# Wo gradient: first operands fetched into the space of the finished row sums, output rows during the weight gradients, SwiGLU backward loads in order of need

## The chip, the cores and the metric

One core of one Trainium2 chip. The metric is the device time of one execution in microseconds (us), lower is better. Medians are over the runs of one kernel.

## The reference, cut to what matters

The program is the forward pass and the gradients of `x + s * g`, where `s` is a recurrent attention with memory over segments of 32 rows (32 heads of 128) and `g` is a SiLU of a SwiGLU block. bfloat16, 2048 rows, width 640, hidden width 1728.

```python
def _fwd_reference(...):
    xn = _layernorm(x)
    s = _A_ref(xn, A_mem0, A_Wq, A_Wk, A_Wv, A_Wo, A_seg_len)    # recurrent, 64 segments of 32 rows
    g = _silu(_B_ref(xn, B_w1, B_w3, B_w2))                     # SwiGLU: (silu(x w1) * (x w3)) w2
    return x + s * g
# outputs: x + s * g (out_0) and the gradients for x, mem0, Wq, Wk, Wv, Wo, w1, w3, w2
```

What follows the recurrent part matters here: the gradients of Wq, Wk, Wv (matmuls `wg`), of Wo (`oa`), of w2 (`w2a`), the SwiGLU backward blocks (`pghb`, `pgxb`), and the gradients of w1 and w3 (`wa`).

## The kernel before: the parts that the change touches

Loads and stores are issued by an engine's queue: `nc.sync` is SP, `nc.scalar` is ScalarE, `nc.gpsimd` is GpSimd. A `tag` names a space in SBUF; a pool's space is free when its `with` block ends. `in_order(k, start)` keeps the instructions of a stage as written, engine by engine; where it is not called, a scheduler chooses their order within each engine.

```python
def phase6_Awgrads(k, out3, out4, out5):           # weight gradients, 8 passes (called quarters) x 22 units
    ...
        hr = hp.tile([120, NTL, D], BF16, name="hr")              # 3.2 MB
        acc = hp.tile([P, NW, D], F32, name="ghacc")              # row sums, 51 KB per partition
        ...
        ld(0); ld_w(0); ld(1); ld(2)     # one statement per line in the kernel
        nc.scalar.dma_start(hr[:, 0:NTL - 1, :], ...)
        ...
        for qd in range(8):
            for tl in range(NTL): ...                             # units
            for i in range(3):
                wg(qd, i) ...                                     # three sweeps of matmuls
        in_order(k, start)

def phase6b_gWo(k, out0, out6, gz):                # Wo gradient
        def ep_ld(tt):
            for nm_, src in (("s", k.SR), ("g", k.GB), ("x", k.A_x), ("G", k.G), ("dz", k.DZ)):
                t_ = io.tile([P, D], BF16, name=f"ep_{nm_}", tag=f"ep_{nm_}")      # two buffers
                nc.gpsimd.dma_start(t_[:], src[rows, :])
        def ep(tt):
            nc.vector.tensor_tensor(g, s, g, ALU.mult)
            nc.vector.tensor_tensor(g, g, x, ALU.add)
            nc.scalar.dma_start(out0f[tt * P:tt * P + P, :], g)                  # output rows
            nc.vector.tensor_tensor(G, G, s, ALU.mult)
            nc.vector.tensor_tensor(gz[:, tt, :], G, dz, ALU.mult)
        ...
        for qd in range(8):
            # orr (2.6 MB) on SP's queue; with qd == 0 also gow (3.3 MB) on ScalarE's queue
            for jp in range(2):
                tt = 2 * qd + jp
                ep_ld(tt + 1)                                     # if there is one
                ep(tt)
                # 80 matmuls oa <- orr, gow; then per head: VectorE and ScalarE copy half
                # of it each to wgoo, SP stores it

def phase5_Bbwd_ln(k, out0, out1, out6, out7, out8, out9):
        for t0 in range(0, NT, 4):
            nc.scalar.dma_start(hb[:, t0:t0 + 4, :], ...)         # 7.1 MB in all
        nc.scalar.dma_start(w2T[:], ...)                          # 2.2 MB
        phase6b_gWo(k, out0, out6, gz)
        ...                                                       # w2a; staging of three buffers
        nc.scalar.dma_start(xn_all[:], ...)                       # 2.6 MB
        for b0 in range(0, S, BLK):                               # eight SwiGLU blocks
            ...   # per pair of chunks: load SLT and DUT tiles (three buffers), pghb matmuls,
            ...   # VectorE: ggT = pghb * du, guT = pghb * sl; then pgxb, transposes, layer norm
```

## Time and profile before

| what | us |
|---|---|
| median | 5746.97 (5737.85 to 5747.56, 4 runs) |
| span of the profiled run | 5743.5 |
| first transpose of the weight gradients (`t`) to first `g` matmul | 42.4 |
| first `g` matmul to the end of the last `wg` | 1470.7 |
| end of the last `wg` to the first `oa` | 53.8 |
| `oa`, first to last | 197.9 |
| to the end of the last `w2a` | 73.7 |
| to the first long run of `pgxb` (the entry of the SwiGLU blocks) | 27.2 |
| SwiGLU blocks, to the first `wa` | 241.8 |
| `wa` to the end | 122.3 |
| sum from the first `t` on | 2229.8 |

The rows are cut where TensorE goes from one kind of matmul to the next, read from its timeline. I use this ledger for every run, because the 3500 us before the first `t` scatter: it began at 3499 to 3532 us in the runs of this study, and no experiment touches what lies ahead of it.

The prediction shows the holes. In the list of waits of VectorE and GpSimd for 5026 to 5280 us (us in total, times, longest), products of the output rows wait for their loads, and a load waits for the store of an older output row:

```profile
DVE ep_g L1489 <- DMA ep_g<-GB: 59.0, 12, 41.9
DVE ep_G L1492 <- DMA ep_s<-SR: 21.5, 11, 5.8
POOL ep_g L1483 <- DMA out_dram<-ep_g: 60.0, 10, 37.9
```

### The profile page before, as it was taken

The numbers are of one execution on the slowest core, as the hardware profiler recorded it, in microseconds if no ns is written. First come the engines' busy times: TensorE is split into PE (matmuls) and PEld (weight loads), VectorE is DVE, ScalarE is ACT, GpSimd is POOL, SyncE is SP. The second block draws the span as 40 slices with busy tenths as digits, with TensorE's granted clock in tenths as the row PEclk, the third lists the DMA queues.
The fourth block names the chain that finished last, engine by engine and source line by source line (L and its number), as shares of the span: only waits on it lengthen the run. The fifth ranks groups of instructions, "written<-read, shape, count | busy, mean of one in ns | idle before, by whom it ended". The sixth has DMA issues, their size and how long they took to land. (4 is left out here: it accounts for less than half of the span.)

```text
span 5743.5 us, 166838 instructions
## 1 busy us (share of the span) xinstructions
PE 5004.5 (87%) x67332; PEld 3202.8 (56%) x67614; DVE 2395.4 (42%) x7479; ACT 1838.9 (32%) x5045; POOL 1530.8 (27%) x2536
## 2 busy tenths in 40 slices
PE   5959799999999775898888986999999999959899
PEld 2536455555555444565556554566556665537565
DVE  5824455555555423444444442233223332221351
ACT  2424355555555422333333322233222322201111
POOL 0000144444444302333333333233223322120000
PEclk9969899999999786999999997999999999979999
DMA  6565355555555565666666655243333433284332
GB/s 221 161 245 197 108 158 157 160 160 157 158 150 147 143 180 160 171 180 186 173 176 176 174 159 116 74 110 91 95 81 93 108 86 83 73 291 134 103 118 89
DMA packets 1011244, 833.21 MB, mean 145 GB/s; under 512 B 506030, under 2 KB 899538, under 8 KB 1007156
## 3 DMA queue, kind: packets, MB, share of 16 engines
q1 hardware_dynamic: 759999, 574.71, 35.6%
q0 software_dynamic: 88176, 133.83, 8.4%
q10 hardware_dynamic: 162297, 113.98, 6.7%
q8 instruction: 533, 8.73, 0.7%
q14 instruction: 239, 1.96, 0.1%
HBM read 509.18 MB, written 324.39 MB: 145 GB/s over the span
## 5 line engine op out<-in xcount | busy, mean ns | idle before, releaser
L1407 PE MATMUL wg<-gr,hr 120*128 120x512 bf16 (+1 forms) x2640 | 590.0, 384 | 17.6 <-DVE dST L1339 12.9
L1385 PE MATMUL g<-w,gT 128*128 128x320 bf16 x3840 | 547.5, 299 | 0.0
L1407 PEld LDWEIGHTS <-hr 120*128 120x128 bf16 (+1 forms) x2640 | 258.3, 99 | 341.3 <-issue 48.5
L1385 PEld LDWEIGHTS <-gT 128*128 128x128 bf16 x3840 | 368.4, 98 | 135.8
L250 POOL DMA_DIRECT2D r<-GOS x256 | 143.0, 561 | 925.3 <-PE r6p L1349 876.3
L373 PEld LDWEIGHTS <-gkv 128*8 128x8 bf16 x8192 | 217.1, 100 | 159.7 <-DVE gkv L1048 35.1
L90 DVE CAST wgo<-wg 128x512 bf16<-128x512 f32 x72 | 47.5, 688 | 585.7 <-PE wg L1407 293.8
L354 PEld LDWEIGHTS <-hx 128*32 128x32 bf16 x7680 | 177.9, 96 | 164.6 <-issue 4.5
L90 DVE CAST stg<-bank 128x512 bf16<-128x512 f32 x256 | 177.2, 692 | 200.3 <-PE bank L354 186.6
L373 PE MATMUL gbank<-WvT,gkv 128*8 128x320 bf16 x4096 | 236.2, 410 | 28.1 <-DVE gkv L1048 28.1
L663 ACT ACTIVATE xP<-xsp,xnm 120x120 bf16<-120x120 f32 (+1 forms) x704 | 240.6, 376 | 10.1 <-DVE xnm L659 5.1
L1518 PE MATMUL oa<-gow,orr 128*128 128x320 bf16 x1280 | 180.9, 305 | 70.8 <-DMA gow<-GWO 55.5
L1394 DVE TENSOR_TENSOR ghacc<-ghacc,g 128x320 f32<-128x320 f32 x240 | 117.2, 488 | 283.8 <-PE g L1385 283.8
L92 ACT CAST wgo<-wg 128x512 bf16<-128x512 f32 x48 | 25.8, 589 | 637.8 <-PE wg L1407 637.8
L1352 ACT CAST gr<-r6p 120x512 bf16<-120x512 f32 (+1 forms) x176 | 103.2, 587 | 373.9 <-PE r6p L1349 337.8
L1185 POOL DMA_DIRECT2D DSR<-gdS x176 | 100.9, 573 | 412.1 <-DVE gdS L1183 391.1
L712 POOL DMA_DIRECT2D OR<-xv x163 | 94.8, 582 | 404.7 <-ACT xv L711 284.9
L92 ACT COPY gT<-t6g 128x960 bf16<-128x960 bf16 (+5 forms) x216 | 167.0, 792 | 111.2 <-PE t6g L1368 110.7
L674 POOL TENSOR_TENSOR xP<-xP,xrz 120x480 bf16<-120x480 bf16 x163 | 161.9, 994 | 140.1 <-ACT xP L663 90.9
L1518 PEld LDWEIGHTS <-orr 128*128 128x128 bf16 x1280 | 127.5, 100 | 124.4 <-issue 72.3
L1183 DVE SCALAR_TENSOR_TENSOR gdS<-gdp,Dx,gPr 120x120 bf16<-120x120 f32 (+1 forms) x704 | 188.8, 330 | 0.0
L1180 DVE CUSTOM_DVE_ANT_0 gdS<-gdp,gPr 120x120 bf16<-120x120 f32 (+1 forms) x704 | 153.7, 274 | 62.3 <-PE gdp L1169 52.2
(335 smaller groups left out, 11113.4 us busy)
## 6 DMA issues: line engine op xcount, KB each, us to landing
QVS<-stg SPq DMA_DIRECT2D x128, 256.0 KB
gqv<-QVS SPq DMA_DIRECT2D x112, 192.0 KB
vTt<-VTD SPq DMA_DIRECT2D x64, 320.0 KB
orr<-OR SPq DMA_DIRECT2D x16, 1280.0 KB
VTD<-gvT POOLq DMA_DIRECT2D x168, 120.0 KB, 3.4
OR<-xv POOLq DMA_DIRECT2D x163, 120.0 KB, 2.6
DSR<-gdS POOLq DMA_DIRECT2D x168, 112.5 KB, 3.2
dS<-DSR SPq DMA_DIRECT2D x168, 112.5 KB
```

The costliest lines, as they stand in the source:

```text
L90: return nc.vector.tensor_copy(out, in_)
L92: return nc.scalar.copy(out, in_)
L250: eng.dma_start(d, src if src.shape[0] > 1 else src[0])
L354: k.nc.tensor.matmul(bank[32 * g:32 * g + 32, :], x[:, dc, :], W[:, dc, c0:c0 + 512], start=(dc == 0), stop=(dc == k.DC - 1), tile_positio ...
L373: k.nc.tensor.matmul(pm[p0:p0 + nq, 0:320], x[:, h, :], W[:, h, 320 * b:320 * b + 320], start=(first and i == 0), stop=(last and i == 15), ...
L663: nc.scalar.activation(Pb[0:n, j, 0:n], sp[0:n, j, :], ACT.Exp, bias=nmx[0:n, j:j + 1], scale=k.scale, accum_out=Z[0:n, j:j + 1])
L674: eng.tensor_tensor(Pb[0:n, :, 0:n], Pb[0:n, :, 0:n], bc_last(rz[0:n], n), ALU.mult)
L1180: nc.vector.tensor_tensor_reduce(dS[0:n, j, :], dp[0:n, j, :], Pr[0:n, j, :], 1.0, 0.0, ALU.mult, ALU.add, Dx[0:n, j:j + 1])
L1183: nc.vector.scalar_tensor_tensor(dS[0:n, j, :], dp[0:n, j, :], Dx[0:n, j:j + 1], Pr[0:n, j, :], op0=ALU.subtract, op1=ALU.mult)
L1385: nc.tensor.matmul(pg[:], ring[:, i, j, r0:r0 + P], Ws[qd][i][:, j, 320 * h:320 * h + 320], start=(i == 0 and j == 0), stop=(i == 2 and j ...
L1407: nc.tensor.matmul(accs[dc][:], hr[0:n, tl, dc * P:(dc + 1) * P], st["g", NTL * qd + tl, i][0:n, :], start=(tl == 0), stop=(tl == NTL - 1))
L1518: nc.tensor.matmul(ac[j][i][:], orr[:, w, jj * P:(jj + 1) * P], gow[:, w, 320 * i:320 * i + 320], start=(w == 0), stop=(w == NW - 1))
```

## The change

Its intent: close TensorE's hole before the Wo gradient by fetching gow and the first orr early, into space that is no longer used (the row sums move to a pool of their own); take work out of that stage that could be done elsewhere (the output rows); and put every large load at the time at which it is needed. The diff, cut to its core:

```diff
 def phase6_Awgrads
-        acc = hp.tile([P, NW, D], F32, name="ghacc")
+        acc = X.tile([P, NW, D], F32, name="ghacc", tag="x")
...
                 s4(u)
+                if tl % 11 == 2:
+                    out_ld(2 * qd + tl // 11)        # s, g, x on GpSimd's queue, one buffer each
+                if tl % 11 == 6:
+                    out_rows(2 * qd + tl // 11)      # two VectorE products, store on GpSimd's queue
...
+            else:                                    # last quarter, ahead of its three sweeps
+                xg = X.tile([P, NW * (D + 512)], BF16, name="xg", tag="x")
+                ...
+                    nc.scalar.dma_start(gow[...])
+                    nc.sync.dma_start(orr[...])
 def phase6b_gWo
-            for nm_, src in (("s", k.SR), ("g", k.GB), ("x", k.A_x), ("G", k.G), ("dz", k.DZ)):
+            for nm_, src in (("s", k.SR), ("G", k.G), ("dz", k.DZ)):
...
+        rows_ld(1)                                   # orr 1; later rows_ld(qd + 2) after each qd
...
                 ep(tt)
+                if qd > 1 and late:
+                    nc.scalar.dma_start(*late.pop(0))  # one of nine slices of hb and w2T
...
+        in_order(k, start)
 def phase5_Bbwd_ln
-            nc.scalar.dma_start(hb[...])             # and w2T: at once, ahead of gow
+            late.append((hb[...]))                   # and w2T: handed to phase6b_gWo
...
-            w1T, w3T, gzT in a pool of their own
+            x5 = X.tile([P, 2 * FC * D + DC * NT * P], BF16, name="x5", tag="x")
...
-                        ot = op.tile([P, 320], BF16, name="w2o", tag="w2o")        # three buffers
+                        ot = op.tile([P, 320], BF16, name="w2o", tag="w2o", bufs=7)
...
-            nc.scalar.dma_start(xn_all[:], ...)
+                        nc.gpsimd.dma_start(xn_all[:, b0 // P:b0 // P + 2, :], ...)  # per block
```

## The prediction

> **What bounds the kernel now.** The change touches only what comes after the recurrent part: the weight gradients (from about 3510 us), the Wo gradient (matmuls named oa), the SwiGLU backward pass (gzp, w2a, pghb, pgxb) and the last two weight gradients (wa). I read the page first for the limiting engine, then the chain of waits from 5000 us on, a table of engine busy time by stage, TensorE's list of waits, and last the timeline around each hole.
>
> ```profile
> PE 5004.5 (87%) x67332; PEld 3202.8 (56%) x67614; DVE 2395.4 (42%) x7479; ACT 1838.9 (32%) x5045; POOL 1530.8 (27%) x2536
> ```
>
> TensorE is the busiest by far; the other engines have more than half the span free. A gain here is a hole of TensorE closed. The stage table puts edges where the matmul groups begin and end:
>
> ```profile
> core 0: us, PE busy (x) PEld busy (x) DVE busy (x) ACT busy (x) POOL busy (x), PEclk, DMA share, GB/s
> 5026.80:5080.60 53.80, 0.00 (x0) 0.02 (x1) 7.09 (x14) 0.44 (x1) 11.81 (x22) 0.52 1.03 368
> 5080.60:5278.50 197.90, 180.91 (x1280) 127.53 (x1280) 38.84 (x83) 11.58 (x31) 30.88 (x58) 0.96 0.56 181
> 5278.50:5352.20 73.70, 70.38 (x529) 46.66 (x528) 10.81 (x24) 10.34 (x20) 0.00 (x0) 1.00 0.28 89
> 5352.20:5367.60 15.40, 2.35 (x11) 1.35 (x10) 1.46 (x5) 0.85 (x2) 0.00 (x0) 0.66 0.73 237
> ```
>
> Row one is the hole between the last weight gradient and the first oa matmul: 53.8 us without a matmul, DMA engines full at 368 GB/s. Row four is a second hole of 15.4 us before the SwiGLU blocks. Who ended them:
>
> ```profile
> PE oa L1518 <- DMA gow<-GWO: 55.5, 2, 53.8
> PE oa L1518 <- DVE wgoo L1523: 15.1, 3, 8.5
> PE pghb L1761 <- DVE w2o L90: 8.1, 1, 8.1
> PE pgxb L1774 <- DVE ggT L1763: 5.8, 2, 5.0
> ```
>
> And why gow came so late (start, duration, engine, instruction, idle before it):
>
> ```profile
> 5026.86 12.41 ACTq L1706 DMA_DIRECT2D hb_all<-HB  x4
> ...
> 5029.34 0.69 DVE L90 CAST wgo<-wg 128x512 bf16<-128x512 f32 x1 [2.04 <-DMA out_dram<-wgo]
> ...
> 5060.20 0.37 ACTq L1708 DMA_DIRECT2D w2T<-W2T  x1
> 5060.61 9.25 ACTq L1506 DMA_DIRECT2D gow<-GWO  x2
> ...
> 5080.61 7.26 PE L1518 MATMUL oa<-gow,orr 128*128 128x320 bf16 x40 [53.84 <-DMA gow<-GWO]
> ...
> 5089.49 20.67 PE L1518 MATMUL oa<-gow,orr 128*128 128x320 bf16 x151 [1.62 <-DMA gow<-GWO]
> ```
>
> No load could start before the weight gradients gave up their space at 5026.8. Then ScalarE's queue took hb (7.1 MB, wanted at 5279) and w2T (2.2 MB, wanted at 5360) ahead of gow (3.3 MB, wanted at once). The first 40 oa matmuls run at 181 ns each, the next 151 at 137 ns: the clock was cold too.
>
> [...] granted clock 0.52 in the long hole, and 181 against 137 ns after it. So a hole costs its length plus a cold start. [...] That bears on the output-row loads, which move into the weight gradients on GpSimd's queue. In the trace such loads beside the same VectorE ops (0.49 us each) land in 2.9 to 6.1 us[...].
>
> **The change part by part.**
>
> (1) gow and the first orr (3.3 + 2.6 MB) go into the space of the row sums ghacc, free once the last row sum is added at about 4955 us. 72 us of weight-gradient matmuls follow, at a DMA share of 0.06. At 368 GB/s they take 16 us: hidden. The listing of the changed kernel's waits shows what the first oa matmul then waits for: these loads, and the evacuation of the last accumulators, the last being VectorE's third wgo copy. Before, that copy ran 5029.34 to 5030.03, because its staging buffer waited 2 us for a store; nothing changes there. New start of oa 5030.1, hole 3.3 us, gain 80.6 - 30.1 = 50.5 us.
>
> (2) Inside oa. 1280 matmuls at 136.9 ns (20.67/151) are 175 us; the stage took 197.9. The 23 us more are the cold start, the second half of gow (1.6 us) and 15.1 us behind VectorE's wgoo copies. [...]its copies stood behind output-row products whose loads waited for stores that had themselves queued on ScalarE behind hb and gow. The change takes those products out (two of four per row tile), fetches only three row loads instead of five, writes the order down, and puts one slice of hb per row tile after the fourth. A row tile lasts 175/16 = 10.9 us and accumulators are double-buffered, so a copy may be late by that much. I leave 1 us for a partly cold start: 176 us, gain 22 us. Does the DMA keep up? In the loaded part per 21.9 us: orr 2.6 MB, hb 1.8, rows 1.0, stores 0.65, so about 6.0 MB, 276 GB/s. That is 75% of the 368 seen. It should hold, with less room than I like.
>
> (3) gzp and w2a: 70.4 busy of 73.7 us. Seven staging buffers instead of three spare most waits for stores; ScalarE has extra loads in its queue, which may give some of it back. Gain 4 us: 73.7 less 448 matmuls at 136.5 ns (61.2), 80 transposes at about 55 ns from their spacing (4.4) and about 4 us of evacuations at group edges.
>
> (4) The 15.4 us hole. Before, evacuation waited for stores in three buffers, 2.6 MB of xn_all stood ahead of the first SLT and DUT tiles, and those could not load before the staging pool closed. After, three pairs of tiles are fetched during w2a, xn_all comes in pieces on GpSimd, and the first pghb waits for seven copies on two engines, about 4 x 0.49 = 2 us, plus 1.4 us of pghb work. Gain 12 us; the cold matmuls after it pay for the wait on the fourth pair.
>
> (5) The weight-gradient stage. New work: 16 x 2 VectorE products at 0.49 us (15.7 us) and 16 x 4 GpSimd issues at 0.54 us (35 us), spread over 1450 us. A unit there lasts 4.77 us with VectorE about half free, and results are needed a unit later: hidden, 2 us lost at most. Also, pools were reordered. In the first 40 us of this stage ScalarE stood still:
>
> ```profile
> 3539.51 0.28 ACTq L1422 DMA_DIRECT2D hr<-HRO  x1
> 3539.84 0.59 ACT L1352 CAST gr<-r6p 120x512 bf16<-120x512 f32 x1 [29.00 <-DMA r<-QVX]
> ```
>
> The second, small hr load sits ahead of that copy in ScalarE's queue. [...]in the listing of before it waits for the one of unit 1's dS, landing behind 2 MB of weights; in the new listing it waits for unit 0's QVX, which lands early. ScalarE is freed, but TensorE then meets unit 1's own dS and QVX, the latter now waiting for hr (3.2 MB). I expect to reach the steady pace 5 us earlier, between 0 and 8.
>
> Sum: 50.5 + 22 + 4 + 12 + 5 - 2 = 91.5 us. 5746.7 - 91.5 = **5655 us**, 1.6% less.
>
> **The rivals.**
>
> *DMA becomes the bound of oa.* hb and w2T left the hole but still have to move, now beside orr. If orr tiles come late, TensorE waits at every change of tile. For it: the first 70 us of oa ran at a DMA share of 0.78 for 247 GB/s, so this mix may top out near 320 GB/s, not 368. Against it: each orr is asked for 22 us ahead. If it happens, four of the later tiles late by 2 to 4 us each, with a cold start now and then, cost 10 to 25 us: 5665 to 5680.
>
> *A new wait takes the hole's place.* Row loads for the first gz tile start only when the weight gradients end, and VectorE must make gz before it evacuates oa. It has 10.9 us; before, such loads landed in 3 to 6. [...]In the SwiGLU entry, ScalarE's queue now holds loads between its copies, one of which waits for all of W1T to land; if TensorE runs into that, part (3) turns into a loss of 3 to 5 us.
>
> *The gain is larger.* All holes closed completely and a full 8 us at the entry give 54 + 24 + 6 + 15 + 8 = 107 us, 5640. Even this is short of 2% (115 us, 5632), so only something outside these stages could pass that line. The earlier parts have the same instruction order in both kernels up to the weight gradients.
>
> *Nothing is gained*, because what is saved is waited for later. Against it: the last stages (pghb blocks 94% busy, then wa) are limited by TensorE, not by the arrival of these bytes, and no load is delayed past its use.
>
> **Range and chances.** The two large terms rest on a measured hole and measured matmul durations and should hold within 6 us together; DMA contention pulls one way, the entry of the weight gradients the other. 8 times in 10 I expect 5638 to 5680. Faster by over 2%: 0.05. Within 2%: 0.94. Slower by over 2%: 0.01.
>
> **What will show it.** Right: TensorE's idle between the last wg and the first oa near 3 us with wgo as releaser; oa in 174 to 180 us without waits for orr; w2a's last matmul to the first pgxb in 3 to 5 us; the first wg matmul of the first quarter up to 8 us earlier. Wrong: waits of oa for orr or for DVE wgoo above 5 us; dS or r waits of TensorE in the weight gradients grown by over 5 us; a granted clock in oa below 0.97; or a change before 3500 us, which would be the state of the run rather than this edit.

## The result, and the profile after

| | before | after |
|---|---|---|
| median, us | 5746.97 | 5656.44 (5646.07 to 5660.46, 4 runs) |
| span of the profiled run, us | 5743.5 | 5658.8 |

The ratio is 0.9843 (95% interval 0.9826 to 0.986): the mean time of the fast runs of one kernel over that of the other's of the same rounds, so not quite the ratio of the medians. The medians differ by 90.5 us, the profiled runs by 84.7. By the ledger, in the profiled runs:

| stage | before | after | change | predicted |
|---|---|---|---|---|
| first `t` to first `g` | 42.4 | 35.1 | -7.3 | -5 |
| `g` to the last `wg` | 1470.7 | 1471.9 | +1.2 | +2 at most |
| hole before `oa` | 53.8 | 2.8 | -51.0 | -50.5 |
| `oa` | 197.9 | 176.6 | -21.3 | -22 |
| to the last `w2a` | 73.7 | 72.8 | -0.9 | -4 |
| entry of the blocks | 27.2 | 21.5 | -5.7 | -12 |
| blocks | 241.8 | 241.8 | 0 | 0 |
| `wa` to the end | 122.3 | 123.0 | +0.7 | 0 |
| sum | 2229.8 | 2145.5 | -84.3 | -91.5 |

The page's line of busy times, to be held against the first line of the prediction, has TensorE busy for 23 us more than before, which fits the 282 more of its matmul records that are there, and its share at 89%:

```profile
PE 5027.7 (89%) x67614; PEld 3200.0 (57%) x67614; DVE 2387.2 (42%) x7479; ACT 1835.1 (32%) x5045; POOL 1552.1 (27%) x2576
```

The table by stage, with the columns of the one in the prediction: the hole, `oa`, `w2a`, and the entry of the blocks (here to the first long run of `pgxb`).

```profile
5020.33:5023.08 2.75, 0.01 (x1) 0.03 (x1) 1.22 (x2) 0.47 (x1) 2.19 (x5) 0.74 0.56 134
5023.08:5199.73 176.65, 176.65 (x1280) 126.23 (x1280) 27.98 (x63) 11.60 (x31) 23.28 (x44) 0.98 0.69 232
5199.73:5272.52 72.79, 70.62 (x528) 46.00 (x528) 10.35 (x25) 10.25 (x22) 0.00 (x0) 1.00 0.36 110
5272.52:5293.99 21.47, 14.27 (x105) 10.29 (x104) 11.21 (x30) 0.37 (x2) 5.66 (x8) 0.84 0.69 212
```

In row two TensorE is busy for the whole of the stage, 176.65 of 176.65 us, at a granted clock of 0.98 and a DMA share of 0.69. Row four is busy for 14.3 of 21.5 us: here the change left something. What TensorE waited for between 4940 and 5320 us (total, times, longest):

```profile
PE pgxb L1811 <- DVE ggT L1800: 5.1, 3, 3.8
PE pghb L1798 <- DVE guT L1801: 3.1, 2, 2.4
PE oa L1550 <- issue: 2.7, 1, 2.7
...
PE pghb L1798 <- DVE w2o L90: 0.9, 1, 0.9
```

The waits for gow (55.5 us) and wgoo (15.1 us) are gone. "issue" is a wait that the profile puts down to nothing; the timelines of ScalarE's queue, VectorE and TensorE show what ended then. gow was issued 72 us ahead of the last `wg`, and the third copy of wgo ended at 5022.98, 0.1 us before the first `oa`:

```profile
4948.41 1.19 ACTq L1491 DMA_DIRECT2D xg<-GWO  x2
```
```profile
5022.29 0.69 DVE L90 CAST wgo<-wg 128x512 bf16<-128x512 f32 x1 [1.43 <-DMA out_dram<-wgo]
```
```profile
5023.08 7.13 PE L1550 MATMUL oa<-xg 128*128 128x320 bf16 x32 [2.74 <-issue]
```

In the entry of the blocks, TensorE's timeline has the first `pgxb` 2.2 us after the last `w2a`, as foreseen, but then two new stalls; the chain of waits names an SLT tile of 9.87 us, and GpSimd's timeline shows all eight pieces of xn_all issued in one go:

```profile
5274.73 0.31 PE L1811 MATMUL pgxb<-x,ggT 128*128 128x320 bf16 x1
...
5283.46 0.31 PE L1811 MATMUL pgxb<-x,ggT 128*128 128x320 bf16 x1 [3.85 <-DVE ggT L1800]
...
5286.22 1.22 PE L1798 MATMUL pghb<-x,w2T 128*128 128x256 bf16 x5 [2.39 <-DVE guT L1801]
```
```profile
5275.85 9.87 DMA sl<-SLT
```
```profile
5273.16 5.66 POOL L1781 DMA_DIRECT2D xn_all<-XN  x8 [103.18 <-DVE w2o L90]
```

The program says "per block", but GpSimd's instructions were not held in written order there.

### The profile page after: what moved, and what is told of

The parts are those of the page before. It is cut to its first block, busy times and chain, and to the rows that moved or that the text cites. A ratio compares the mean times of both kernels' runs of the same rounds, so it can differ in the third digit from the quotient of the medians.

```text
span 5658.8 us, 167048 instructions
## 1 busy us (share of the span) xinstructions
PE 5027.7 (89%) x67614; PEld 3200.0 (57%) x67614; DVE 2387.2 (42%) x7479; ACT 1835.1 (32%) x5045; POOL 1552.1 (27%) x2576
## 5 line engine op out<-in xcount | busy, mean ns | idle before, releaser
L373 PEld LDWEIGHTS <-gkv 128*8 128x8 bf16 x8192 | 213.6, 98 | 155.7 <-DVE gkv L1048 35.0
L92 ACT CAST wgo<-wg 128x512 bf16<-128x512 f32 x48 | 25.8, 589 | 637.2 <-PE wg L1409 637.2
L1155 POOL DMA_DIRECT2D VTD<-gvT x176 | 129.5, 740 | 176.4 <-ACT gvT L1154 151.9
L1370 PE MATMUL t6g<-ident,gr 120*128 120x120 bf16 (+1 forms) x2112 | 171.4, 220 | 3.3 <-DVE wgo L90 2.7
```

The lines of the kernel that those rows point to most:

```text
L92: return nc.scalar.copy(out, in_)
L373: k.nc.tensor.matmul(pm[p0:p0 + nq, 0:320], x[:, h, :], W[:, h, 320 * b:320 * b + 320], start=(first and i == 0), stop=(last and i == 15), ...
L1370: nc.tensor.transpose(pt[:, i - i0, j, :], st["g", u, i][0:n, j * P:(j + 1) * P], k.ident[0:n, 0:n])
```

## The experiments

Ledgers of the profiled runs (us; `t`-`g`, then `g` to the last `wg`, hole, `oa`, `w2a`, entry, blocks, and all from the first `t` to the end), with the median and the ratio to the runs of before on the same chip:

| kernel | t-g | wg | hole | oa | w2a | entry | blocks | from t | median | ratio (95%) |
|---|---|---|---|---|---|---|---|---|---|---|
| before | 42.4 | 1470.7 | 53.8 | 197.9 | 73.7 | 27.2 | 241.8 | 2229.8 | 5746.97 | |
| after | 35.1 | 1471.9 | 2.8 | 176.6 | 72.8 | 21.5 | 241.8 | 2145.5 | 5656.44 | 0.9843 (0.9826-0.986) |
| order_only | 42.4 | 1469.4 | 25.2 | 213.6 | 70.7 | 27.4 | 243.1 | 2214.9 | 5725.67 | 0.9971 (0.9955-0.9988) |
| order_spread | 42.4 | 1473.9 | 25.3 | 202.8 | 72.5 | 27.8 | 243.6 | 2212.0 | 5719.79 | 0.9945 (0.9927-0.9963) |
| late_fetch | 36.1 | 1471.9 | 23.4 | 175.8 | 73.0 | 21.4 | 243.8 | 2166.6 | 5676.57 | 0.9885 (0.9868-0.9903) |
| rows_back | 36.6 | 1467.6 | 2.7 | 174.0 | 71.8 | 21.5 | 242.9 | 2140.0 | 5657.43 | 0.9856 (0.984-0.9871) |
| hb_at_once | 35.2 | 1469.6 | 2.8 | 180.1 | 72.8 | 21.3 | 241.1 | 2145.8 | 5657.80 | 0.9853 (0.9836-0.987) |
| w2o_three | 35.9 | 1473.2 | 2.8 | 175.4 | 72.6 | 19.8 | 242.7 | 2145.5 | 5656.49 | 0.9836 (0.9818-0.9855) |
| xn_by_block | 36.3 | 1472.5 | 2.7 | 175.7 | 72.2 | 13.0 | 252.0 | 2147.1 | 5659.32 | 0.9844 (0.9825-0.9863) |
| xn_block_b4 | 35.8 | 1475.2 | 2.7 | 175.7 | 72.6 | 12.7 | 239.8 | 2136.4 | 5649.45 | 0.9838 (0.9818-0.9858) |
| hr_late | 21.2 | 1478.0 | 2.7 | 175.3 | 72.0 | 21.6 | 241.7 | 2135.6 | 5645.07 | 0.9822 (0.9801-0.9843) |
| best | 21.4 | 1476.1 | 2.7 | 175.7 | 73.0 | 13.1 | 255.7 | 2139.1 | 5656.34 | 0.9836 (0.9819-0.9854) |
| hr_rows | 21.6 | 1475.0 | 2.7 | 174.0 | 72.2 | 21.5 | 244.1 | 2132.6 | 5640.06 | 0.9818 (0.9796-0.9839) |
| hr_rows_xn | 21.4 | 1473.7 | 2.7 | 175.7 | 73.1 | 12.7 | 239.1 | 2119.7 | 5629.91 | 0.9816 (0.9795-0.9836) |

All gave correct results. Where nothing of a stage was edited, it repeats within about 2 us (hole, `oa`, `w2a`), 3 us (blocks) and 6 us (`wg`: 1469.6 to 1475.2); smaller differences are not read. The medians of before themselves lie between 5737.7 and 5748.2 us from one group of runs to the next, so medians of different chips are read only beside the ledger.

### order_only: the order of the loads alone

Theory: most of the hole was hb and w2T standing ahead of gow. Rival: only the early space helps.

```diff
 # from the kernel before
-        nc.scalar.dma_start(hb[...]) ; nc.scalar.dma_start(w2T[...])     # ahead of phase6b_gWo
+        # collected in late, and in phase6b_gWo after gow and the first orr are issued:
+            if qd == 0:
+                for d in late:
+                    nc.scalar.dma_start(*d)
```

> From the kernel before: only the order of loads on ScalarE's queue changes; hb and w2T (9.3 MB) are issued after gow and the first orr instead of ahead of gow. No space is freed earlier. Theory 'order' (most of the 53.8 us hole was the 9.3 MB standing ahead): gow and orr are 5.9 MB, at the 368 GB/s of the hole 16 us, plus some 2 us of start and a first half of gow that may land sooner, so the hole falls to 12 to 22 us and the kernel gains 32 to 50 us of the 90 (hole, plus part of the 15 us that oa waited for VectorE). Theory 'space' (only fetching during the weight gradients helps): the hole stays over 40 us and the gain is under 15 us.

Measured: the hole fell by 28.6 us to 25.2, but `oa` grew by 15.7. The median gain is 19 us (5745.07 to 5725.67), between the two expectations; the hole, too, is 3 us over the range. TensorE's timeline shows the first tile of orr, and then its second half, awaited:

```profile
5045.59 6.86 PE L1521 MATMUL oa<-gow,orr 128*128 128x320 bf16 x40 [25.22 <-DMA orr<-OR]
5062.26 20.65 PE L1521 MATMUL oa<-gow,orr 128*128 128x320 bf16 x140 [9.81 <-DMA orr<-OR]
```

What follows: the hole that is left is not hb's doing, for the next run, in which hb comes much later, has 25.3 us of it. What hb costs are the 9.8 us after it, which that run does not have. The second half of the first orr was issued on SP's queue at 5030.4 and hb on ScalarE's at 5033.7, 3.3 us later, and yet hb still delays orr. A place further back in another queue did not take these 9.3 MB out of the way (9.8 us of waiting); a later time did (no wait for that half in order_spread). VectorE's copies were also still awaited, 17.1 us.

### order_spread: order, and the large load in slices

```diff
 # from the kernel before: hb and w2T as nine entries of late
                 ep(tt)
+                if qd > 1 and late:
+                    nc.scalar.dma_start(*late.pop(0))
...
+        in_order(k, start, mybir.EngineType.Activation)     # ScalarE alone in written order
```

> From the kernel before: gow and the first orr first, as in order_only, but hb and w2T are then loaded in nine slices, one per row tile from the fourth on, with ScalarE's instructions of this stage in written order. The output rows stay where they were and nothing is fetched early. Theory (in order_only 9.3 MB right behind gow only moved the wait to the second orr, 25 of the 46 us that hole and oa could lose were byte time that has to be spread out): hole 23 to 26 us as in order_only and late_fetch, oa 175 to 182 us without waits for orr, VectorE's 17 us gone with the queue they stood in, total 42 to 55 us faster than the kernel before. Rival (the products of the output rows or the unwritten order of VectorE keep the 15 us): oa 190 us or more, total under 40 us faster.

Measured: `oa` waited for orr no more, except for the hole itself, and gained 10.8 us over order_only. But it took 202.8 us, not 175 to 182: the theory fails and the rival holds. 25 us by medians (5744.98 to 5719.79) is all. TensorE waited 17.2 us for VectorE's wgoo, now in eight waits of at most 3.7 us:

```profile
PE oa L1524 <- DVE wgoo L1529: 17.2, 8, 3.7
```

I had expected them to vanish with the queue in which the output rows' stores stood. Two timelines show what they are. VectorE first, one and a half row tiles:

```profile
5084.33 0.88 DVE L1529 CAST wgoo<-oa 128x320 bf16<-128x320 f32 x2
5092.24 0.49 DVE L1493 TENSOR_TENSOR ep_g<-ep_s,ep_g 128x640 bf16<-128x640 bf16 x1 [7.03 <-DMA ep_g<-GB]
...
5096.07 0.49 DVE L1496 TENSOR_TENSOR ep_G<-ep_G,ep_s 128x640 bf16<-128x640 bf16 x1 [2.81 <-DMA ep_s<-SR]
...
5097.00 0.88 DVE L1529 CAST wgoo<-oa 128x320 bf16<-128x320 f32 x2
```

and GpSimd, which issues the loads, at the same time:

```profile
5084.70 0.54 POOL L1487 DMA_DIRECT2D ep_G<-in_grad_out_dram  x1 [6.21 <-DVE gz_all L1497]
...
5085.76 0.54 POOL L1487 DMA_DIRECT2D ep_g<-GB  x1
5093.03 0.54 POOL L1487 DMA_DIRECT2D ep_s<-SR  x1 [6.74 <-DVE ep_g L1493]
```

It is a ring. VectorE's product at 5092.24 waits for the load issued at 5085.76; GpSimd's next load, at 5093.03, waits for that product; the product at 5096.07 waits for that load. Two round trips, with waits of 3 to 8 us, per row tile, and the copies of wgoo stand behind them in VectorE's order. VectorE's first products of a row tile follow each other at 11.0 to 15.8 us here, where the matmuls of one row tile take 10.9 us. From its issue to the product that waits for it a load takes 6.5 and 3.0 us in these lines, 2.7 to 7.2 us from 5061 to 5119 us; it is asked for too late, in the order that the scheduler gave GpSimd and VectorE. No store of ScalarE's queue is in this stretch of the ring; GpSimd's four waits for one (24.8 us) ended at 5054.6 and from 5205.4 on.

### rows_back: the output rows back in the Wo-gradient stage

```diff
 # from the changed kernel
-                if tl % 11 == 2: out_ld(...)        # and out_rows(...)
-            for nm_, src in (("s", k.SR), ("G", k.G), ("dz", k.DZ)):
+            for nm_, src in (("s", k.SR), ("g", k.GB), ("x", k.A_x), ("G", k.G), ("dz", k.DZ)):
+            nc.vector.tensor_tensor(g, s, g, ALU.mult)
+            nc.vector.tensor_tensor(g, g, x, ALU.add)
+            nc.scalar.dma_start(out0f[tt * P:tt * P + P, :], g)
```

> From the changed kernel: the output rows go back into the Wo-gradient stage (five row loads instead of three, four VectorE products per row tile instead of two, the store on ScalarE's queue). Theory A (before, the products were late because their loads and stores queued behind hb and gow, and that queue is gone now): oa 177 to 181 us, total within 4 us of the changed kernel. Theory B (the two extra products per row tile in VectorE's order, 16 x 2 x 0.49 = 16 us, are themselves what held the copies of wgoo): waits of oa for VectorE of 10 to 15 us, oa 188 to 193 us, total 10 to 16 us slower.

Measured: `oa` 174.0 us, no shorter with the products out than in. Median 5657.43 against 5656.44: the same. The weight gradients took 4.3 us less without the moved rows, within what their stage repeats to. Theory A's total held (its `oa` came 3 us under the range given), and theory B is out. VectorE does the same four products per row tile as in order_spread, from the same two buffers, now behind one another and, after the first row tile, with no wait, and the copies come as soon as TensorE is done:

```profile
5040.87 0.89 DVE L1554 CAST wgoo<-oa 128x320 bf16<-128x320 f32 x2 [6.43 <-PE oa L1549]
5041.67 0.48 DVE L1516 TENSOR_TENSOR ep_g<-ep_s,ep_g 128x640 bf16<-128x640 bf16 x1
...
5043.11 0.49 DVE L1520 TENSOR_TENSOR gz_all<-ep_G,ep_dz 128x640 bf16<-128x640 bf16 x1
5051.73 0.89 DVE L1554 CAST wgoo<-oa 128x320 bf16<-128x320 f32 x2 [8.13 <-PE oa L1549]
```

The 2.6 us by which `oa` is shorter than in the changed kernel are the start of TensorE. In the changed kernel the first 32 matmuls take 223 ns each (7.13 us, shown above) at a granted clock of 0.62 (0.50 in the first 3.5 us, 0.74 in the rest), the later ones 136 ns; here, after the same pause of 2.7 us, they take 136 ns from the first. Of the ten runs with this pause eight start cold and two (this one and hr_rows) do not.

What follows: moving the output rows, the most visible part of the edit, is worth nothing here. What the stage needed was its written order. One thing stays open: rows_back also differs from order_spread by the early fetch and by orr being asked for two tiles ahead. Once it ran, order_spread waited for VectorE and not for orr, and late_fetch, below, has an `oa` of 175.8 us without the early fetch. So I take the order for the cause, but it is argued and not shown alone: a kernel before with VectorE and GpSimd alone put in order was not run.

### late_fetch: gow and the first orr only after the last weight gradient

```diff
 # from the changed kernel: the four dma_start of gow and orr moved behind
             for i in range(3):
                 wg(qd, i)
                 ...
+        # here, after the last sweep
```

> From the changed kernel: gow and the first orr are issued after the last weight gradient instead of during the last three sweeps; their space is still that of the row sums, hb and w2T still come in slices later. Theory (early fetch is worth what 5.9 MB take): the hole grows from 2.7 to 14 to 20 us and oa starts at a cold clock (up to 5 us more), total 13 to 23 us slower than the changed kernel. Rival (the order of the loads alone did it, and the fetch would be hidden anyway by the evacuation of the last accumulators): hole under 8 us, total under 6 us slower.

Measured: the hole is 23.4 us, 3 us over the range, in one wait for orr; `oa` did not lengthen (175.8).

```profile
PE oa L1550 <- DMA xg<-OR: 23.4, 1, 23.4
```

21.1 us more from the first `t`, 20 us by medians. So the early fetch is worth 20 us, given the rest, not 50.

Read in a row, hole and `oa` together take 251.7 us before, 238.8 with the order of loads (-12.9), 228.1 with slices (-10.7), 199.2 with the stage in written order, orr two ahead and the rows out (-28.9; rows_back says that the rows are nothing of it), and 179.4 with the early fetch (-19.8).

### hb_at_once: hb and w2T in one burst at the start of the Wo gradient

```diff
-                if qd > 1 and late:
+                while late:
                     nc.scalar.dma_start(*late.pop(0))
```

> From the changed kernel: hb and w2T (9.3 MB) are all issued at the first row tile of the Wo gradient instead of in nine slices from the fourth on. Theory 'room' ([...]a tile of orr is asked for 22 us ahead): oa stays within 177 +- 2 us. Rival 'DMA bound': 9.3 + 2.6 MB at about 320 GB/s are 37 us, so the second orr, wanted 22 us later, comes 5 to 15 us late, with a wait of oa for orr in the list and a cold clock after it; total 5 to 18 us slower.

Measured: `oa` 180.1 us, 3.5 more, of which one wait of TensorE for orr is 2.6. Medians 5657.80 and 5656.44, no difference that the runs resolve. Between the two theories: with gow and orr already there, a burst of 9.3 MB is nearly hidden. The slices are cheap insurance, not the gain. In order_only the same burst cost more (9.8 us for the second half of the first orr, which was still on its way).

### w2o_three: three staging buffers again

```diff
-                            ot = op.tile([P, 320], BF16, name="w2o", tag="w2o", bufs=7)
+                            ot = op.tile([P, 320], BF16, name="w2o", tag="w2o", bufs=3)
```

> From the changed kernel: the staging buffers of w2o go back from seven to three. Theory (the copies of w2a waited for stores): gzp and w2a stay at 72 to 74 us, for ScalarE's queue limits there, and the first pghb comes 2 to 6 us later after w2a; total 2 to 6 us slower. Rival (buffers did not matter): total within 1 us.

Measured: median 5656.49 against 5656.44, from the first `t` 2145.5 both: the rival. `w2a` is as long (72.6). The mechanism of the theory is there all the same: the first `pghb` now waits 6.6 us for a copy, against 0.9,

```profile
5282.49 3.36 PE L1798 MATMUL pghb<-x,w2T 128*128 128x256 bf16 x15 [6.58 <-DVE w2o L90]
```

but the two later stalls of 3.85 and 2.39 us are gone, for the SLT tile that they wait for comes no earlier. Seven buffers remove a wait ahead of a wait for the same late data.

### xn_by_block and xn_block_b4: xn_all in pieces that are really issued per block

```diff
 # from the changed kernel: xn_by_block
+                    start = len(nc.cur_bb.bb.instructions)          # ahead of the blocks
...
+                    in_order(k, start, mybir.EngineType.Pool)       # GpSimd alone in written order
 # xn_block_b4, in addition
-                            sl, du: bufs=3
+                            sl, du: bufs=4
```

> From the changed kernel: the GpSimd engine's instructions of the SwiGLU blocks are put in written order, so that the eight pieces of xn_all (2.6 MB) are issued one per block instead of all at once when w2a ends. Theory (the burst of 2.6 MB delays the fourth pair of SLT and DUT tiles, for which the chain shows 9.87 us): the stretch from the last w2a to the first full pgxb run falls from 21.5 to 13 to 17 us, total 4 to 8 us faster. Rival (the fourth pair is late because its buffer comes free only when the first pair has been used, whatever else moves): stretch 20 to 22 us, total within 2 us.

Measured for xn_by_block: the entry fell to 13.0 us, as the theory has it, but the blocks grew by 10.2 us, and the total did not move (5659.32). Given back later: each block's piece of xn_all now runs against that block's own SLT and DUT tiles (the next run tests this). VectorE's waits for the two, from 5270 to 5545 us, were 13.8 us in the changed kernel (7.8 for DUT, 6.0 for SLT, the longest at the entry). Here they are 15.4: 0.3 for SLT, and for DUT no wait over 2.3 us, but nine of them:

```profile
DVE ggT L1803 <- DMA du<-DUT: 15.1, 9, 2.3
```

Counted in the blocks alone, from the first long run of `pgxb` to the first `wa`, they are 7.4 us in the changed kernel and 15.0 here, and TensorE's waits for VectorE's products behind them grow from 10.8 to 17.3 us: some two thirds of the 10.2.

> From the changed kernel: xn_by_block with four instead of three buffers for the pairs of SLT and DUT tiles. In xn_by_block the 8.5 us won at the entry came back as 1.3 us per block, where VectorE waited for DUT (9 waits, 15.1 us). Theory (each block's piece of xn_all delays that block's own pairs, and one more pair of lead hides it): entry 12 to 14 us, blocks to wa 241 to 245 us, total 4 to 8 us faster than the changed kernel. Rival (the order of GpSimd's own work is what costs, or the lead is not the limit): blocks stay at 250 us or more, total within 3 us.

Measured for xn_block_b4: entry 12.7, blocks 239.8, so 10.9 us less for the two than in the changed kernel; 9.1 us less from the first `t`. The median, 5649.45, is 7 us lower, though the ratios' intervals overlap. In the same view of the waits, taken 20 us later since this run reached the blocks later, VectorE's for DUT are down to 4.3 us:

```profile
DVE ggT L1803 <- DMA du<-DUT: 4.3, 6, 1.3
```

The theory holds: the burst delays the fourth pair at the entry; spread out, it needs one more pair of lead. Four buffers with the burst left in were not run.

### hr_late: hr out of the entry of the weight gradients

```diff
 # from the changed kernel
-        nc.scalar.dma_start(hr[:, 0:NTL - 1, :], ...)               # 3.2 MB, ahead of the units
+                if qd == 0 and tl in (1, 5, 9, 13):
+                    nc.scalar.dma_start(hr[:, t0:t1, :], ...)       # a quarter of it
```

> From the changed kernel: hr (3.2 MB) is loaded in four pieces during the first quarter of the weight gradients instead of at its start. Theory (at the entry TensorE waits for dS and QVX behind hr and the weights; hr is 3.2 MB, at 368 GB/s about 9 us): the time from the first t matmul to the first g matmul, 35 us now, falls by 7 to 15 us, and the total by the same. Rival (the weights are ahead of dS anyway[...]): falls by under 3 us.

Measured: first `t` to first `g` 21.2 us instead of 35.1, inside the theory's range. In the list of waits from just before the first `t` to the first `g`, TensorE's longest was 16.8 us in the changed kernel and is 8.8 now, for the same dS tile of the second unit; the first line is the changed kernel, the second this one:

```profile
PE t L1339 <- DMA dS<-DSR: 20.4, 2, 16.8
```
```profile
PE t L1339 <- DMA dS<-DSR: 13.6, 3, 8.8
```

The 9 us counted for hr are at the 368 GB/s of the hole of before (share 1.03, 576 of 10366 packets under 512 bytes). At this entry, from 3510 to 3548 us in the changed kernel, the DMA moved a mean of 220 GB/s at a share of 1.06, with 6426 of 12130 packets under 512 bytes. No run here isolates the packet size as the cause.

6.1 of the 13.9 us come back in the rest of the stage (4.2 in best, which has the same edit), about what that stage repeats to; the pieces run beside the units' loads there, but no run shows that this is the reason. From the first `t` it is 9.9 us, by medians 11.4; the intervals of the ratios overlap.

### best, hr_rows, hr_rows_xn: what adds up

best is hr_late with xn_by_block; hr_rows is hr_late with rows_back; hr_rows_xn is hr_rows with xn_block_b4. Their edits are those above.

> Both edits at once, hr late and xn_all by block, on the changed kernel. If both theories hold and the gains add: 11 to 23 us faster than the changed kernel, about 5633 to 5645 us. If neither holds: within 3 us of 5656.

> From the changed kernel: hr in four pieces later, as in hr_late, and the output rows back in the Wo-gradient stage, as in rows_back. If the two are independent: first t to first g matmul near 21 us, weight gradients 1495 to 1500 us in all, oa 174 to 178 us, total 10 to 17 us faster than the changed kernel. If taking 16 x 4 transfers out of the weight gradients does nothing: as hr_late, 8 to 11 us faster.

> hr_rows with the entry of xn_block_b4: three independent edits on the changed kernel. hr_rows was 5640 us, and xn_block_b4 took 11 us off the stretch from the last w2a to the first wa (252.4 against 263.3 us in the profiles). If the gains add: 5626 to 5634 us, ratio to the kernel before 0.978 to 0.981, clearly under the changed kernel's 0.984. If the late hr and the blocks share a limit that only shows elsewhere: 5640 us or more.

Measured: best was no better than the changed kernel (5656.34), for it took xn_by_block's give-back with it (blocks 255.7); that expectation was a miss. hr_rows came to 5640.06, in its range. hr_rows_xn came to 5629.91, in its range by the median; its ratio of 0.9816 is just outside the one I had given, as the runs of before were fast on that chip too (5737.71). From the first `t` it is 25.8 us under the changed kernel (2119.7 against 2145.5): 13.7 at the entry of the weight gradients, 11.5 at the SwiGLU blocks with their entry, and under 2 us elsewhere. Its slowest run (5644.09) is under the changed kernel's fastest (5646.07), though in another group of runs; the intervals of the ratios (0.9795 to 0.9836 and 0.9826 to 0.986) still overlap a little.

## Why the prediction was right or wrong

The predicted 5655 us met a median of 5656.4. A little of that is luck: by the ledger the sum is 84.3 and not 91.5 us, and items (3) and (4) promised 9.4 us that did not come.

(1) The hole: 51.0 for 50.5, with the releaser foreseen (the third copy of wgo). Right in size. But the reason counted in item (1), that the early fetch hides these loads, is only part of it: late_fetch puts 20 us on it. The remaining 30 are hb and w2T having left the hole, which the prediction saw ("ahead of gow") but did not count apart. The 368 GB/s at which item (1) counts these loads are no ceiling: they are the mean of the hole, in which the DMA moved 388 GB/s from 5033 to 5058 us.

(2) `oa`: 21.3 for 22. Right in size. The step "behind output-row products whose loads waited for stores that had themselves queued on ScalarE behind hb and gow" is the one that failed as a cause. It was true of the one long wait of before, which lay mostly in the hole. TensorE's three waits for wgoo (5.1, 8.5 and 1.5 us) ended at 5121.9, 5143.0 and 5158.4, when hb and gow had long been issued (the last at 5069.9). I had also overlooked VectorE's order there. Between these two pairs of copies

```profile
5121.37 0.88 DVE L1523 CAST wgoo<-oa 128x320 bf16<-128x320 f32 x2
...
5142.44 0.88 DVE L1523 CAST wgoo<-oa 128x320 bf16<-128x320 f32 x2
```

stand sixteen products, those of four row tiles: 7.9 us of work and a further 12 us of waits for loads, where the matmuls of one row tile take 10.9 us. The last product ends at 5157.9, and from 5158.9 TensorE runs 119.6 us without a wait. The experiments agree: order_spread kept 17.2 us of waits without that queue, and rows_back, with the stage in written order, had none with all products in place. The order of VectorE and GpSimd is, as far as these runs show, what carries the gain; the prediction named it ("writes the order down") without counting it. The 1 us left for a cold start was an estimate; it measured 2.6 in the profiled run and nothing in two others (rows_back, hr_rows), after a pause of 2.7 us in all three.

(3) `w2a`: 0.9 for 4, mis-sized. "Seven staging buffers instead of three spare most waits for stores" is not what shows: w2o_three took as long. The sum also asked for too much: by the prediction's own table TensorE was busy for 70.4 of the 73.7 us, so at most 3.3 us were there to gain (after: 70.6 of 72.8).

(4) The entry of the blocks: 5.7 for 12, mis-sized. The first `pgxb` came 2.2 us after `w2a`, against the 3.4 us worked out and 15.4 before, so 13.2 us were won; but from there to the first long run of `pgxb` it took 19.3 us instead of 11.8. "xn_all comes in pieces on GpSimd" was the mistake: the pieces were issued together, and the wait on the fourth pair was not paid for by the cold matmuls alone (after the stalls, from 5286.2 to 5291.4 us, the granted clock was 0.51), as I had it, but by 6.2 us of new stalls. xn_block_b4 shows the 12 us to have been there (27.2 to 12.7).

(5) The weight gradients: 7.3 for 5 at their entry, with dS behind the weights and hr as the wait that follows; +1.2 for at most +2 after it, which is less than the stage repeats to. One of the prediction's signs of being wrong did come: TensorE's waits for dS in this stage grew from 19.1 to 39.0 us. But those for ScalarE's gr of line 1352 (1354 after) fell from 27.2 to 6.5, so one wait took the other's place, as item (5) has it, and the sign was drawn too tight. The loads of the moved output rows landed in 2.1 to 5.6 us there, none later than such loads before (the 2.9 to 6.1 us of the prediction are medians; single loads took 2.3 to 9.0).

The 1.6% is within the 2% to which the prediction gave 0.94. The rivals: DMA did not become the bound of `oa`, though hb_at_once shows it near (2.6 us of wait for orr). The new wait at the SwiGLU entry came, in another place than the one named, and smaller than the one it replaced.

## What to carry to other kernels

A load that was in the way was not out of the way in another queue (9.8 us of waiting in order_only): give it a later time (none in order_spread). Before moving work off an engine, look at whether that engine waits for loads that another engine issues too late (17.2 us of TensorE's waits for wgoo in order_spread, none in rows_back); writing the order down may give the same gain for nothing, and where order matters and is not written, read it from the trace. Spread a burst only with enough buffers for what it then runs beside, or its cost comes back in small waits (xn_by_block: 8.5 us less at the entry, 10.2 more in the blocks; with a fourth buffer 10.9 less for the two).
